# A mixer block on one core: another order for the first tiles, one tile transposed by DMA, one copied in halves

## The chip, the cores and the metric

The kernel runs on one core of a Trainium2 chip. The metric is the device time of one execution in microseconds; for the kernel before it is the median of three runs. A core has TensorE (PE, matmuls and transposes into PSUM), VectorE (DVE), ScalarE (ACT), GpSimd (POOL) and SyncE (SP, which here only issues DMAs). Each engine works through its own list of instructions in order and waits on semaphores for the others.

## The reference

One layer of an MLP-mixer on 2048 tokens of 512 channels, all bf16, cut to what matters:

```python
h  = gelu(layernorm(x) @ w1)                    # w1: 512 x 512
g0, g1, g2, g3 = four channel groups of h, shifted along the tokens by +1, -1, +2, -2
x1 = x + concat(g0, g1, g2, g3) @ w2            # w2: 512 x 512
out = x1 + gelu(layernorm(x1) @ w3) @ w4        # w3: 512 x 1792, w4: 1792 x 512
```

## The kernel before, in words

The tokens are split into 16 tiles of 128 (tile t holds the tokens 16p + t, one per partition p). A shift by one or two tokens is then mostly a neighbouring tile, so a tile of the second product needs hidden tiles up to two places away on either side. The second half of the kernel works in the order 8, 9, ..., 15, 0, ..., 7.

A matmul contracts over partitions, so each tile of x must be transposed (xnT) before the first product. There are two ways through the first layer:

- Raw tiles 0 to 5: the tile of x is transposed as it is, by PE (`tp`, four 128x128 transposes into PSUM, L323) with a copy by ScalarE (`ev`, L332), or, for tiles 4 and 5, by a transposing DMA from HBM (`tdma_x`, L351). Then four 128x512 matmuls (`m1r`, L378) and a ScalarE copy of the product to SBUF (`rc`, L388). The layer norm is put in later, from the column sums of w1 (`cs0` to `cs`, four 128x512 matmuls with a matrix of ones, L366, copied out by `cse`).
- Normalised tiles 6 to 15, in pairs: VectorE takes statistics (`st`, L289) and aggregates them (`ag`, L294), GpSimd takes the root (`rs`, L300), VectorE normalises (`nm`, L309). The pair is transposed by PE (pairs 8 and 10: `tp`, eight transposes, and one `ev` of 1024 columns) or by a transposing DMA from SBUF (pairs 6, 12, 14: `td0`, L343). Then 16 matmuls of 128x256 (`m1p`, L410) and a gelu by ScalarE (`g1p`, or `g1s` by single tiles for pair 10).

The second product (`m2`, L436 and L450) adds into x1 on VectorE (`x1`, L460); its parts for tiles 8 to 15 are cut into pieces by which hidden tiles they read. The third and fourth products (`m3h` L492, `m3` L468, `m4` L511) are long runs of PE work.

Ahead of everything PE runs a warm-up of matmuls on constants (`wu`, L534), while the first loads are under way.

What sets the order: a small `Program` class holds named operations with what they read and write. For each engine a list `firsts[...]` written out by hand gives the order of its first operations; those not named follow in the order in which they were added. `emit` derives the semaphore waits from reads and writes. SP's list matters as much as PE's: it issues nearly all loads and all transposing DMAs, in order, and an issue that waits for its data (`td0_6` waits for `nm0_6` and `nm0_7`) holds those behind it. PSUM has eight banks; a product can start only when the copy or gelu that emptied its bank is done.

Of the kernel before, what the change touches and what calls it, by code (L numbers as in the profile page):

```python
# [26 lines left out]
class Program:  # L27
# [7 lines left out]
    def add(self, eng, name, fn, reads=(), writes=(), dma=False):  # L35
        self.ops.append(Op(name, eng, fn, reads, writes, dma))
# [135 lines left out]
def bass_standalone__mixer_s_mlp__prompt_kernel(nc: bass.Bass, x, w1, w2, w3, w4, out):  # L172
# [4 lines left out]
    DC = D // P  # L177
# [5 lines left out]
    xd = x[0].rearrange("(p t) d -> p t d", t=NT)  # L183
# [4 lines left out]
    with ExitStack() as es:  # L188
        sb = lambda name, shape, dt: es.enter_context(nc.sbuf_tensor(name, shape, dt))
        x_sb = sb("x_sb", [P, NT, D], BF16)  # L190
# [3 lines left out]
        xnT = sb("xnT", [P, NT, DC, P], BF16)  # L194
# [21 lines left out]
        ones_wide = nc.const_aps.tensor(1.0, [P, 512], BF16)  # L216
# [66 lines left out]
        def dst_of(layer, t):  # L283
            return (xn, t, ("xn", t), 0) if layer == 0 else (x1n, POS[t] % 8, ("x1n", POS[t] % 8), t)
# [29 lines left out]
        def tp(t, n, b, raw):  # L314
            src = x_sb if raw else xn
            rd = [(("x", i), 0) if raw else (("xn", i), 0) for i in range(t, t + n)]

            def f(e):
                ins = None
                for i in range(n):  # L320
                    for c in range(DC):
                        o = 1024 * b + (i * DC + c) * P
                        ins = e.transpose(psb[:, o : o + P], src[:, t + i, P * c : P * (c + 1)], ident[:])  # L323
# [12 lines left out]


        def tdma(layer, t, n):
# [3 lines left out]
            add("sp", f"td{layer}_{t}",  # L342
                lambda e: e.dma_start(dst[:, p0 : p0 + n, :, :].rearrange("p t c s -> p (t c) s"),  # L343
                                      src[:, k : k + n, :].rearrange("p t d -> p (t d)"), transpose=True),
                reads=[dst_of(layer, i)[2:] for i in range(t, t + n)],
                writes=[(("xT", i) if layer == 0 else ("x1T", i), 0) for i in range(t, t + n)], dma=True)


        def tdma_x(t):
            add("sp", f"tdx_{t}",  # L350
                lambda e: e.dma_start(xnT[:, t : t + 2, :, :].rearrange("p t c s -> p (t c) s"),  # L351
                                      xd[:, t : t + 2, :].rearrange("p t d -> p (t d)"), transpose=True),
                writes=[(("xT", i), 0) for i in (t, t + 1)], dma=True)
# [20 lines left out]
        def m1r(t, b, c0=0, c1=DC):  # L374
            def f(e):
                ins = None
                for c in range(c0, c1):
                    ins = e.matmul(bank(b), xnT[:, t, c, :], w1_sb[:, c, :], start=(c == 0), stop=(c == DC - 1))  # L378
                return ins

            rd = [(("xT", t), 0)] + W1[c0:c1]
            if c0:
                rd += bres(b, 1, f"m1r{t}{c0}")
            end = f"{c1}" if c1 < DC else ""
            add("pe", f"m1r{t}{end}", f, reads=rd, writes=bres(b, 1, f"m1r{t}{end}"))

        def rc(t, b):
            add("act", f"rc{t}", lambda e: e.activation(yraw[:, t, :], bank(b), ACT_F.Copy),  # L388
                reads=bres(b, 1, f"m1r{t}"), writes=[(("yraw", t), 0)])
# [140 lines left out]
        def warmup(name, n, b):  # L530
            def f(e):
                ins = None
                for _ in range(n):
                    ins = e.matmul(bank(b), ones, ones_wide, start=True, stop=True)  # L534
                return ins

            add("pe", name, f, writes=bres(b, 1, name))
# [5 lines left out]
                writes=[(("w1", c), 0)], dma=True)  # L543

        def load_w2(c):
            add("sp", f"ldw2{c}", lambda e: e.dma_start(w2_sb[:, c, :], w2[P * c : P * (c + 1), :]),
                writes=[(("w2", c), 0)], dma=True)

        def load_w3a(c):
            add("sp", f"ldw3a{c}",  # L550
# [11 lines left out]
        load_w1(2, "act")  # L562
        load_w1(3, "sp")
        load_x(1, 1, "act")
        for t, n in ((6, 1), (7, 1), (2, 1), (8, 1), (3, 1), (9, 1), (10, 1), (11, 1), (12, 1), (13, 1), (14, 2), (4, 2)):
            load_x(t, n)
        for c in range(DC):
            load_w2(c)
        for c in range(DC):
            load_w3a(c)  # L570
        load_w3b()

        warmup("wu", 7, 5)
        YB = (0, 1, 2, 3, 0, 1)
        for c in range(DC):
            colsum(4, c)
        colsum_out(4)
        for t in range(R):
            if t < 4:
                tp(t, 1, 6 + t % 2, True)  # L580
                ev(t, 1, 6 + t % 2, "act")
            elif t == 4:
                tdma_x(t)
            cuts = [0, 1, 2, 3, 4] if t == 0 else [0, 2, 4] if t == 1 else [0, 4]
            for c0, c1 in zip(cuts, cuts[1:]):
                m1r(t, YB[t], c0, c1)
            rc(t, YB[t])
# [7 lines left out]
        for t in range(R, NT, 2):  # L595
# [2 lines left out]
                ev(t, 2, 6 + t // 2 % 2)  # L598
            else:
                tdma(0, t, 2)  # L600
        for t, b in ((6, 2), (8, 4), (10, 0), (12, 2), (14, 6)):
            m1p(t, b)
            if t == 10:
                g1s(t, b, 0)
                g1s(t, b, 1)
            else:
                g1p(t, b)
# [19 lines left out]
        for t in (8, 10):  # L627
# [7 lines left out]
            tdma(1, t, 2)  # L635

        firsts = {}
        firsts["pe"] = """wu tp0 cs0 cs1 m1r01 m1r02 tp1 m1r03 cs2 m1r0 cs tp2 m1r12 m1r1 tp3 m1r2 m1r3 m1r4 m1r5 tp8 m1p6
            tp10 m1p8 m1p10 m2_8a m2_9a m2_8 m2_9b m2_9 m2_10a m2_11a m2_12a m2_13a m1p12 m1p14 m2_10 m2_11
            m2_12b m2_13b m2_14a m2_15a m2_12 m2_13 m2_14b m2_15b m2_14 m2_15""".split()  # L640
        firsts["act"] = """ldw10 ldw12 ldx1 table ev0 ev1 rc0 ev2 ev3 rc1 rc2 rc3 rc4 rc5 ev8 cse g1p6 ev10 g1p8 g1s10 g1s11
            g1r0 g1r1 g1p12 g1p14 g2h_0_0_0 g2h_0_0_4 g1r2 g1r3 g2h_0_0_8 g2h_0_0_12 g1r4 g1r5""".split()
        firsts["dve"] = """pada padb padc padd pade padf st0_0 st0_6 st0_7 ag0_6 ag0_7
            st0_8 nm0_6 nm0_7 st0_9 ag0_8 ag0_9 st0_10 st0_11 nm0_8 nm0_9 ag0_10 ag0_11
            st0_12 nm0_10 nm0_11 st0_13 ag0_12 ag0_13 st0_14 st0_15 ag0_14 ag0_15 nm0_12 nm0_13 st0_1 ag0_0 ag0_1
            nm0_14 nm0_15 zr0 zr1 x1_8 x1_9 st1_8 st1_9 ag1_8 ag1_9 st0_2 nm1_8 nm1_9 st0_3 ag0_2 ag0_3 x1_10 x1_11 st1_10
            st1_11 ag1_10 ag1_11 x1_12 nm1_10 nm1_11 x1_13 x1_14 x1_15 zr2 zr3 st0_4 st0_5 ag0_4 ag0_5 zr4 zr5
            st1_12 st1_13 ag1_12 ag1_13""".split()
        firsts["pool"] = """ident0 ident1 neghalf stz ste rs0_6 rs0_8 rs0_10
            rs0_12 rs0_14 rs0_0 rs1_8 rs0_2 rs1_10""".split()  # L650
        firsts["sp"] = """ldx0 ldw11 ldx6 ldw13 ldx7 ldx2 ldx8 ldx3 ldx9 tdx_4 ldx10 ldx11 ldx12 td0_6 ldx13 ldx14 ldw20 ldw21 ldw22 ldw23 td0_12 td0_14 ldw3a0 ldw3a1
            ldw3a2 ldw3a3 th_0 td1_8 ldw3b ldx4 td1_10 th_2 th_4 td1_12 td1_14 ldw4""".split()

        slots = [4, 0, 2]
        ns = [0]
# [54 lines left out]
        for i, t in enumerate((0, 1, 2, 3, 4, 5, 6, 7)):  # L710
            b = (6, 7, 1)[i % 3]
# [54 lines left out]
```

## Time and profile before

| what | us |
|---|---|
| median of 3 runs | 136.76 (136.42, 136.76, 136.97) |
| the profiled execution | 136.32 |
| its span, first to last instruction | 134.5 |
| PE busy | 130.8 (97%) |
| VectorE busy | 58.3 (43%) |
| ScalarE busy | 46.8 (35%) |
| GpSimd busy | 12.5 (9%) |

The profiled execution is the only one of which the order of work in time is known; it was 0.44 us faster than the median. Busy time of PE includes the drain of each matmul, so 97% says that PE has hardly a pause, not that each matmul is at its fastest. A matmul is recorded with the time to its end (0.38 us for 128x512), while the next one starts one slot later (0.216 us). A few matmul records are missing from the trace. Times inside the span count from its start.

### The profile page before, as it was taken

The numbers are of one execution on the slowest core, as the hardware profiler recorded it, in microseconds if no ns is written. First come the engines' busy times: TensorE is split into PE (matmuls) and PEld (weight loads), VectorE is DVE, ScalarE is ACT, GpSimd is POOL, SyncE is SP. The second block draws the span as 40 slices with busy tenths as digits, with TensorE's granted clock in tenths as the row PEclk, the third lists the DMA queues.
The fourth block names the chain that finished last, engine by engine and source line by source line (L and its number), as shares of the span: only waits on it lengthen the run. The fifth ranks groups of instructions, "written<-read, shape, count | busy, mean of one in ns | idle before, by whom it ended". The sixth has DMA issues, their size and how long they took to land.

```text
span 134.5 us, 1794 instructions
## 1 busy us (share of the span) xinstructions
PE 130.8 (97%) x719; PEld 69.6 (52%) x729; DVE 58.3 (43%) x135; ACT 46.8 (35%) x56; POOL 12.5 (9%) x25
## 2 busy tenths in 40 slices
PE   7999999999999999999999999999999999999993
PEld 2446857678884444444444444444444444444452
DVE  0689999799967777762222000122200002322222
ACT  3488871507962036550001555200066630000000
POOL 2042422220330012220000000000000000000000
PEclk9999999999999999999999999999999999999999
DMA  4999379984465984444121000011110001111121
GB/s 123 317 247 217 115 145 246 255 292 83 78 128 100 295 262 78 78 80 78 39 68 49 5 0 0 0 39 39 41 37 5 0 0 39 39 39 39 44 75 42
DMA packets 24376, 12.96 MB, mean 96 GB/s; under 512 B 16688, under 2 KB 23600, under 8 KB 24368
## 3 DMA queue, kind: packets, MB, share of 16 engines
q1 hardware_dynamic: 23792, 12.42, 36.5%
q10 hardware_dynamic: 576, 0.43, 1.0%
q8 instruction: 6, 0.10, 0.3%
q14 instruction: 2, 0.02, 0.1%
HBM read 6.82 MB, written 2.10 MB: 66 GB/s over the span
## 4 chain that ended last, share of the span: by engine, by line
PE 89%; SPq 4%; DMA 2%; DVE 2%; issue 1%
PE ps L511 36%; PE ps L468 27%; PE ps L492 9%; PE ps L410 7%; PE ps L436 5%; PE ps L450 5%; DMA x_sb<-in_x_dram 2%; SPq L272 2%; SPq L351 1%; DVE st L289 1%; PE ps L323 1%; SPq L542 1%; DVE xn L309 0%; DVE o_sb L523 0%
## 5 line engine op out<-in xcount | busy, mean ns | idle before, releaser
L511 PE MATMUL ps<-w_sb,h2T 128*128 128x512 bf16 (+2 forms) x232 | 48.1, 366 | 0.3
L523 DVE TENSOR_TENSOR o_sb<-ps,x_sb 128x512 bf16<-128x512 f32 (+2 forms) x17 | 11.2, 660 | 61.2 <-PE ps L511 61.2
L479 ACT ACTIVATE h2T<-ps 128x1024 bf16<-128x1024 f32 x21 | 21.5, 1023 | 46.2 <-PE ps L468 46.2
L468 PE MATMUL ps<-x1nT,w_sb 128*128 128x512 bf16 x168 | 36.7, 379 | 0.0
L511 PEld LDWEIGHTS ps<-w_sb,h2T 128*128 128x128 bf16 x238 | 22.8, 98 | 25.9
L468 PEld LDWEIGHTS ps<-x1nT,w_sb 128*128 128x128 bf16 x168 | 16.4, 98 | 19.8
L289 DVE BATCH_NORM_STATS2 st<-x_sb 128x6 f32<-128x512 bf16 x32 | 20.9, 682 | 4.1 <-DMA x_sb<-in_x_dram 4.0
L300 POOL TENSOR_TENSOR rstd<-mv,neghalf 128x2 f32<-128x2 f32 x16 | 11.6, 725 | 46.1 <-DVE mv L294 46.1
L492 PE MATMUL ps<-x1nT,w_sb 128*128 128x256 bf16 x112 | 12.4, 273 | 0.0
L492 PEld LDWEIGHTS ps<-x1nT,w_sb 128*128 128x128 bf16 x112 | 11.0, 98 | 1.5
L460 DVE TENSOR_TENSOR x_sb<-ps,x_sb 128x512 bf16<-128x512 f32 x16 | 10.6, 685 | 2.5 <-PE ps L436 1.5
L410 PE MATMUL ps<-xnT,w_sb 128*128 128x256 bf16 x80 | 9.2, 273 | 0.0
L503 ACT ACTIVATE h2T<-ps 128x1024 bf16<-128x1024 f32 (+1 forms) x8 | 7.1, 913 | 6.0 <-PE ps L492 6.0
L410 PEld LDWEIGHTS ps<-xnT,w_sb 128*128 128x128 bf16 x80 | 7.6, 98 | 1.2
L309 DVE TENSOR_SCALAR x1n<-x_sb,mv,rstd 128x512 bf16<-128x512 bf16 x16 | 5.9, 409 | 5.3 <-POOL rstd L300 5.3
L450 PE MATMUL ps<-w_sb,hTf 128*128 128x512 bf16 x30 | 7.0, 379 | 0.1
L436 PE MATMUL ps<-w_sb,hTf 128*128 128x512 bf16 x31 | 6.9, 379 | 0.1
L378 PE MATMUL ps<-w_sb,xnT 128*128 128x512 bf16 x23 | 6.0, 382 | 0.1
L420 ACT ACTIVATE hTf<-ps 128x1024 bf16<-128x1024 f32 x4 | 4.1, 1023 | 4.2 <-PE ps L410 4.2
L332 ACT ACTIVATE xnT<-ps 128x512 bf16<-128x512 bf16 (+1 forms) x6 | 4.4, 738 | 2.3 <-PE ps L323 2.2
L436 PEld LDWEIGHTS ps<-w_sb,hTf 128*128 128x128 bf16 x32 | 3.1, 98 | 3.6
L294 DVE BATCH_NORM_AGGREGATE mv<-st 128x2 f32<-128x9 f32 x32 | 5.0, 185 | 0.0
(28 smaller groups left out, 36.8 us busy)
## 6 DMA issues: line engine op xcount, KB each, us to landing
out_dram<-o_sb SPq DMA_DIRECT2D x15, 128.0 KB, 1.8
w_sb<-in_w_dram SPq DMA_DIRECT2D x1, 1792.0 KB, 7.7
x_sb<-in_x_dram SPq DMA_DIRECT2D x11, 128.0 KB, 3.3
w_sb<-in_w_dram SPq DMA_DIRECT2D x4, 256.0 KB, 4.2
w_sb<-in_w_dram SPq DMA_DIRECT2D x6, 128.0 KB, 3.5
w_sb<-in_w_dram SPq DMA_DIRECT2D x1, 768.0 KB, 4.8
x_sb<-in_x_dram SPq DMA_DIRECT2D x2, 256.0 KB, 4.4
w_sb<-in_w_dram ACTq DMA_DIRECT2D x2, 128.0 KB, 3.2
```

Of the source, the lines that this page charges most:

```text
L289: add("dve", f"st{layer}_{t}", lambda e: e.bn_stats(st9[:, i, 0:6], src[:, t, :]), reads=[(r, 0)], writes=[(("st6", i), 0)])
L300: lambda e: e.tensor_tensor(rstd[:, i : i + n], mv[:, i : i + n, 1], neghalf[:, 0:n], ALU.pow),
L410: ins = e.matmul(dst, w1_sb[:, c, P * fc : P * (fc + 1)], xnT[:, t : t + 2, c, :], start=(c == 0), stop=(c == DC - 1))
L436: ins = e.matmul(bank(b), hTf[:, c0 : c0 + P], w2_sb[:, j, :], start=(j == 0), stop=(j == DC - 1))
L450: ins = e.matmul(bank(b), hTf[:, w[0] : w[0] + P], w2_sb[:, j, :], start=first and n == 0, stop=last and n == len(js) - 1)
L460: lambda e: e.tensor_tensor(x1_sb[:, t, :], bank(b), x_sb[:, t, :], ALU.add),
L468: ins = e.matmul(bank(b), w3_sb[:, c, P * fc : P * (fc + 1)], x1nT[:, 4 * q : 4 * q + 4, c, :], start=(c == 0), stop=(c == DC - 1))
L479: lambda e: e.activation(h2T[:, fc : fc + 2, q % 2, :], src, ACT_F.Gelu_apprx_tanh),
L492: ins = e.matmul(dst, w3_sb[:, c, P * (fc + i) : P * (fc + i + 1)], x1nT[:, t : t + 2, c, :], start=(c == 0), stop=(c == DC - 1))
L503: lambda e: e.activation(h2T[:, fc : fc + n, q % 2, 256 * k : 256 * (k + 1)], src, ACT_F.Gelu_apprx_tanh),
L511: ins = e.matmul(ps[:, 512 * b : 512 * b + c1 - c0], h2T[:, fc, q % 2, P * i : P * (i + 1)], w4_sb[:, fc, c0:c1], start=(fc == 0), stop=(f ...
L523: lambda e: e.tensor_tensor(o_sb[:, k % 4, c0:c1], ps[:, 512 * b : 512 * b + c1 - c0], x1_sb[:, t, c0:c1], ALU.add),
```

## The change

In words:

- The warm-up is 14 matmuls of 256 columns instead of 7 of 512.
- Tile 0 is transposed and copied in two halves (`tp0a`/`ev0a` into bank 6, `tp0b`/`ev0b` into bank 7); its first two matmuls read only the first half.
- Tile 3 is transposed by a DMA from HBM of its own (`tdx_3`), ahead of the one for tiles 4 and 5. Its own load (`ldx3`, still wanted by the statistics and by x1) moves behind pair 14's transpose.
- Tiles 8 and 9 are loaded ahead of 6 and 7; pair 8 is normalised first, transposed behind `m1r3`, and multiplied (`m1p8`) ahead of pair 10's transposes and of `m1p6`. The PSUM banks of the two products are exchanged.
- The last column sum (`cs`) moves from behind `m1r0` to behind `m1r2`; tile 1's transposes stand behind `m1r03`.
- Tiles 12 and 13 are one load, 14 and 15 two; tile 15's comes right behind pair 6's transpose. w2 comes in two loads instead of four. Two of the four first parts of w3 are issued ahead of pair 12's transpose.

```diff
+        def tp_part(t, c0, c1, b, part, res):
...
+            add("pe", f"tp{t}{part}", f, reads=[(("x", t), 0), ("ident", 1)], writes=bres(b, 1, f"tp{t}{part}"))
+            add("act", f"ev{t}{part}",
+                lambda e: e.activation(xnT[:, t, c0:c1, :].rearrange("p c s -> p (c s)"), psb[:, o : o + n], ACT_F.Copy),
+                reads=bres(b, 1, f"tp{t}{part}"), writes=[(res, 0)])
...
-            rd = [(("xT", t), 0)] + W1[c0:c1]
+            rd = [(("xTa", t) if t == 0 and c1 <= 2 else ("xT", t), 0)] + W1[c0:c1]
...
-                    ins = e.matmul(bank(b), ones, ones_wide, start=True, stop=True)
+                    ins = e.matmul(ps[:, 512 * b : 512 * b + 256], ones, ones_wide, start=True, stop=True)
...
-        for t, n in ((6, 1), (7, 1), (2, 1), (8, 1), (3, 1), (9, 1), (10, 1), (11, 1), (12, 1), (13, 1), (14, 2), (4, 2)):
+        for t, n in ((8, 1), (6, 1), (7, 1), (2, 1), (3, 1), (9, 1), (10, 1), (11, 1), (12, 2), (14, 1), (15, 1), (4, 2)):
             load_x(t, n)
-        for c in range(DC):
+        for c in range(0, DC, 2):
             load_w2(c)
...
-        warmup("wu", 7, 5)
+        warmup("wu", 14, 5)
...
-            if t < 4:
+            if t == 0:
+                tp_part(0, 0, 2, 6, "a", ("xTa", 0))
+                tp_part(0, 2, 4, 7, "b", ("xT", 0))
+            elif t < 3:
                 tp(t, 1, 6 + t % 2, True)
                 ev(t, 1, 6 + t % 2, "act")
-            elif t == 4:
-                tdma_x(t)
+            elif t < 5:
+                tdma_x(t, 1 if t == 3 else 2)
...
-        for t, b in ((6, 2), (8, 4), (10, 0), (12, 2), (14, 6)):
+        for t, b in ((6, 4), (8, 2), (10, 0), (12, 2), (14, 6)):
...
-        firsts["pe"] = """wu tp0 cs0 cs1 m1r01 m1r02 tp1 m1r03 cs2 m1r0 cs tp2 m1r12 m1r1 tp3 m1r2 m1r3 m1r4 m1r5 tp8 m1p6
-            tp10 m1p8 m1p10 m2_8a m2_9a m2_8 ...
+        firsts["pe"] = """wu tp0a tp0b cs0 cs1 m1r01 m1r02 m1r03 tp1 m1r0 cs2 tp2 m1r12 m1r1 m1r2 cs m1r3 tp8 m1r4 m1r5
+            m1p8 tp10 m1p6 m1p10 m2_8a m2_9a m2_8 ...
-        firsts["act"] = """ldw10 ldw12 ldx1 table ev0 ev1 rc0 ev2 ev3 rc1 rc2 rc3 rc4 rc5 ev8 cse g1p6 ev10 g1p8 g1s10 g1s11
+        firsts["act"] = """ldw10 ldw12 ldx1 table ev0a ev0b ev1 ev2 rc0 rc1 rc2 rc3 ev8 rc4 rc5 cse ev10 g1p8 g1p6 g1s10 g1s11
...
-        firsts["dve"] = """pada padb padc padd pade padf st0_0 st0_6 st0_7 ag0_6 ag0_7
-            st0_8 nm0_6 nm0_7 st0_9 ag0_8 ag0_9 st0_10 st0_11 nm0_8 nm0_9 ag0_10 ag0_11
-            st0_12 nm0_10 nm0_11 st0_13 ag0_12 ag0_13 st0_14 st0_15 ag0_14 ag0_15 nm0_12 nm0_13 st0_1 ag0_0 ag0_1
+        firsts["dve"] = """pada padb padc padd pade padf st0_0 st0_8 ag0_8 st0_9 ag0_9
+            st0_6 st0_7 ag0_6 ag0_7 nm0_8 nm0_9 nm0_6 nm0_7 st0_10 st0_11 ag0_10 ag0_11
+            st0_12 nm0_10 nm0_11 st0_13 ag0_12 ag0_13 st0_14 nm0_12 nm0_13 st0_15 ag0_14 ag0_15 st0_1 ag0_0 ag0_1
...
-        firsts["pool"] = """ident0 ident1 neghalf stz ste rs0_6 rs0_8 rs0_10
+        firsts["pool"] = """ident0 ident1 neghalf stz ste rs0_8 rs0_6 rs0_10
...
-        firsts["sp"] = """ldx0 ldw11 ldx6 ldw13 ldx7 ldx2 ldx8 ldx3 ldx9 tdx_4 ldx10 ldx11 ldx12 td0_6 ldx13 ldx14 ldw20 ldw21 ldw22 ldw23 td0_12 td0_14 ldw3a0 ldw3a1
-            ldw3a2 ldw3a3 th_0 td1_8 ldw3b ldx4 td1_10 th_2 th_4 td1_12 td1_14 ldw4""".split()
+        firsts["sp"] = """ldx0 ldw11 ldx8 ldw13 ldx9 ldx2 ldx6 ldx7 tdx_3 tdx_4 ldx10 ldx11 ldx12 ldx14 td0_6 ldx15 ldw20 ldw22 ldw3a0 ldw3a1 td0_12 td0_14 ldx3 ldw3a2
+            ldw3a3 th_0 td1_8 ldw3b ldx4 td1_10 th_2 th_4 td1_12 td1_14 ldw4""".split()
```

More of the change, by code (lines that the diff above doesn't have):

```diff
@@ L215, in bass_standalone__mixer_s_mlp__prompt_kernel @@
         ones = nc.const_aps.tensor(1.0, [P, P], BF16)
-        ones_wide = nc.const_aps.tensor(1.0, [P, 512], BF16)
+        ones_wide = nc.const_aps.tensor(1.0, [P, 256], BF16)
         one_f = nc.const_aps.tensor(1.0, [P, 1], F32)
@@ L335, in ev, with f @@
             add(eng, f"ev{t}", f, reads=bres(b, 1, f"tp{t}"), writes=[(("xT", i), 0) for i in range(t, t + n)])
+        def tp_part(t, c0, c1, b, part, res):
+            o = 1024 * b
+            n = (c1 - c0) * P
+            def f(e):
+                ins = None
+                for c in range(c0, c1):
+                    k = o + (c - c0) * P
+                    ins = e.transpose(psb[:, k : k + P], x_sb[:, t, P * c : P * (c + 1)], ident[:])
+                return ins
+            add("pe", f"tp{t}{part}", f, reads=[(("x", t), 0), ("ident", 1)], writes=bres(b, 1, f"tp{t}{part}"))
+            add("act", f"ev{t}{part}",
+                lambda e: e.activation(xnT[:, t, c0:c1, :].rearrange("p c s -> p (c s)"), psb[:, o : o + n], ACT_F.Copy),
+                reads=bres(b, 1, f"tp{t}{part}"), writes=[(res, 0)])
         def tdma(layer, t, n):
@@ L346, in tdma, with tdma_x @@
                 writes=[(("xT", i) if layer == 0 else ("x1T", i), 0) for i in range(t, t + n)], dma=True)
-        def tdma_x(t):
+        def tdma_x(t, n):
             add("sp", f"tdx_{t}",
-                lambda e: e.dma_start(xnT[:, t : t + 2, :, :].rearrange("p t c s -> p (t c) s"),
-                                      xd[:, t : t + 2, :].rearrange("p t d -> p (t d)"), transpose=True),
-                writes=[(("xT", i), 0) for i in (t, t + 1)], dma=True)
+                lambda e: e.dma_start(xnT[:, t : t + n, :, :].rearrange("p t c s -> p (t c) s"),
+                                      xd[:, t : t + n, :].rearrange("p t d -> p (t d)"), transpose=True),
+                writes=[(("xT", i), 0) for i in range(t, t + n)], dma=True)
         def tdma_h(t, n):
@@ L545, in load_w2 @@
         def load_w2(c):
-            add("sp", f"ldw2{c}", lambda e: e.dma_start(w2_sb[:, c, :], w2[P * c : P * (c + 1), :]),
-                writes=[(("w2", c), 0)], dma=True)
+            add("sp", f"ldw2{c}",
+                lambda e: e.dma_start(w2_sb[:, c : c + 2, :],
+                                      w2[P * c : P * (c + 2), :].rearrange("(c p) f -> p c f", p=P)),
+                writes=[(("w2", c + i), 0) for i in range(2)], dma=True)
         def load_w3a(c):
@@ L637, in bass_standalone__mixer_s_mlp__prompt_kernel @@
         firsts = {}
-        firsts["pe"] = """wu tp0 cs0 cs1 m1r01 m1r02 tp1 m1r03 cs2 m1r0 cs tp2 m1r12 m1r1 tp3 m1r2 m1r3 m1r4 m1r5 tp8 m1p6
-            tp10 m1p8 m1p10 m2_8a m2_9a m2_8 m2_9b m2_9 m2_10a m2_11a m2_12a m2_13a m1p12 m1p14 m2_10 m2_11
+        firsts["pe"] = """wu tp0a tp0b cs0 cs1 m1r01 m1r02 m1r03 tp1 m1r0 cs2 tp2 m1r12 m1r1 m1r2 cs m1r3 tp8 m1r4 m1r5
+            m1p8 tp10 m1p6 m1p10 m2_8a m2_9a m2_8 m2_9b m2_9 m2_10a m2_11a m2_12a m2_13a m1p12 m1p14 m2_10 m2_11
             m2_12b m2_13b m2_14a m2_15a m2_12 m2_13 m2_14b m2_15b m2_14 m2_15""".split()
-        firsts["act"] = """ldw10 ldw12 ldx1 table ev0 ev1 rc0 ev2 ev3 rc1 rc2 rc3 rc4 rc5 ev8 cse g1p6 ev10 g1p8 g1s10 g1s11
+        firsts["act"] = """ldw10 ldw12 ldx1 table ev0a ev0b ev1 ev2 rc0 rc1 rc2 rc3 ev8 rc4 rc5 cse ev10 g1p8 g1p6 g1s10 g1s11
             g1r0 g1r1 g1p12 g1p14 g2h_0_0_0 g2h_0_0_4 g1r2 g1r3 g2h_0_0_8 g2h_0_0_12 g1r4 g1r5""".split()
-        firsts["dve"] = """pada padb padc padd pade padf st0_0 st0_6 st0_7 ag0_6 ag0_7
-            st0_8 nm0_6 nm0_7 st0_9 ag0_8 ag0_9 st0_10 st0_11 nm0_8 nm0_9 ag0_10 ag0_11
-            st0_12 nm0_10 nm0_11 st0_13 ag0_12 ag0_13 st0_14 st0_15 ag0_14 ag0_15 nm0_12 nm0_13 st0_1 ag0_0 ag0_1
+        firsts["dve"] = """pada padb padc padd pade padf st0_0 st0_8 ag0_8 st0_9 ag0_9
+            st0_6 st0_7 ag0_6 ag0_7 nm0_8 nm0_9 nm0_6 nm0_7 st0_10 st0_11 ag0_10 ag0_11
+            st0_12 nm0_10 nm0_11 st0_13 ag0_12 ag0_13 st0_14 nm0_12 nm0_13 st0_15 ag0_14 ag0_15 st0_1 ag0_0 ag0_1
             nm0_14 nm0_15 zr0 zr1 x1_8 x1_9 st1_8 st1_9 ag1_8 ag1_9 st0_2 nm1_8 nm1_9 st0_3 ag0_2 ag0_3 x1_10 x1_11 st1_10
```

## Prediction, before the result was known

> **What bounds the kernel now.** I read the page's chain of waits by share first, then the chain in order of time, then the timeline of the first 18 us, and last the DMA view, the whole and in windows around single issues.
>
> ```profile
> PE 89%; SPq 4%; DMA 2%; DVE 2%; issue 1%
> ...
> 4.97 1.40 SPq L351
> 6.37 0.05 issue
> 6.42 3.24 DMA x_sb<-in_x_dram
> 9.66 0.02 issue
> 9.68 1.29 DVE st L289 x2
> 10.97 0.64 DVE xn L309 x2
> 11.61 0.05 issue
> 11.66 0.62 PE ps L323 x8
> 12.28 1.81 PE ps L410 x16
> 14.09 0.45 PE ps L323 x8
> 14.53 3.50 PE ps L410 x32
> ```
>
> The chain leaves TensorE (PE) once: SyncE's issues (SPq) up to tile 10's load, its landing at 9.66, its statistics, the normalising of pair 8, and at 11.66 pair 8's transposes. From there to 132 the chain is PE without a gap over 0.05 us. Whatever the change does after 12 us is free as long as its data come in time; what it can win lies in the first 12 us.
>
> ```profile
> 3.71 0.63 PE L323 MATMUL ps<-ident,x_sb 128*128 128x128 bf16 x4
> 4.14 1.06 PE L366 MATMUL ps<-w_sb,const-bfloat16-1.0 128*128 128x512 bf16 x2
> 7.70 0.39 PE L323 MATMUL ps<-ident,x_sb 128*128 128x128 bf16 x4
> 7.93 3.62 PE L378 MATMUL ps<-w_sb,xnT 128*128 128x512 bf16 x15
> 8.41 1.24 SPq L343 DMA_TRANSPOSE xnT<-xn  x1
> 11.65 0.45 PEld L323 LDWEIGHTS ps<-ident,xn 128*128 128x128 bf16 x8 [0.61 <-DVE xn L309]
> 12.16 1.92 PE L410 MATMUL ps<-xnT,w_sb 128*128 128x256 bf16 x16
> ```
>
> Prices from these rows: a warm 128x512 matmul has a slot of 0.216 us (chain: L468 x56 in 12.09), a 128x256 one 0.109 (x32 in 3.50), four 128x128 transposes 0.22 (7.70 to 7.93). Tiles 2 to 5 are 16 matmuls from 7.93 (one record is missing), so they end at 11.39; pair 8's transposes start at 11.66: PE stands still for 0.28. Pair 6's DMA transpose, issued at 8.41, lands after 3.7, at 12.12, and m1p6 starts at 12.16: no slack there either, 0.05 lost. m1p10 ends at 17.85.
>
> ```profile
> x_sb<-in_x_dram SPq DMA_DIRECT2D x11, 128.0 KB, 3.3
> xnT<-xn SPq DMA_TRANSPOSE x3, 3.2
> xnT<-in_x_dram SPq DMA_TRANSPOSE x1, 4.3
> ```
>
> These are the times from issue to landing that I use below.
>
> **The change part by part.**
>
> Warm-up: 7 matmuls of 512 columns become 14 of 256. The weight loads of the first 3.7 us start 0.43 apart, twice the later slot, so the array is at half speed there, and 14 x 0.213 = 7 x 0.427 = 2.99 us. Its weight loads of 0.15 hide in 0.213. Price 0; bounds -0.1 (tile 0 may start at 3.58 instead of 3.71, x0 having landed by 3.57) and +0.1.
>
> Tile 0 in halves: ScalarE copies 512 columns in 0.60 and 1024 in 1.02, so 256 take about 0.39. First half 4.18 to 4.57, second to 4.85, against one copy 4.38 to 4.98. But cs0 and cs1 occupy PE from 4.14 at 0.427 each, to 4.99; m1r01 began at 5.03. Gain 0.04; the colsums cover the rest.
>
> Tile 3: its four transposes go, -0.22 on PE, and one copy of 0.60 on ScalarE, off the path. In their place SP issues a transpose of one tile from HBM, ninth in its queue, at about 4.5. Its issue time and landing are not in the trace. Issue: between a load's 0.43 and the two-tile transpose's 1.40; I take 0.9, half-way. Landing: it queues behind tile 7, which will land near 7.5 to 7.8 (the loads in those two places, tiles 3 and 9, landed at 7.52 and 8.21), plus half of the 1.07 by which the two-tile transpose followed tile 9 (9.28 - 8.21): 8.1 to 8.4; the far bound is the whole 4.31, 8.8. [...] Pair 4's transpose comes at 5.4 instead of 4.97 and lands at 9.2 to 9.9.
>
> PE order, slot by slot: cs1 ends 4.99; m1r01 (part of it still slow, 0.28), m1r02, m1r03 to 5.75; tile 1 transposed to 5.98; m1r0 and cs2 to 6.41; tile 2 lands at 6.48, its transposes 6.52 to 6.75 (0.11 lost); m1r12 needs ev1, whose source is ready near 6.19 and which takes 0.60: 6.82 (0.08 lost). Before, m1r0 and two colsums lay between tile 1's transposes and this point, now less does. m1r1, m1r2, cs are 9 slots: 8.77. m1r3 wants tile 3 at 8.77 (slack 0.4 to 0.7 by the estimate, 0 at the far bound). 9.63 pair 8's transposes, m1r4 at 10.08, m1r5 ends 11.80, m1p8 13.55, pair 10's transposes 14.00, m1p6 15.74, m1p10 17.49.
>
> VectorE order (statistics 0.69, 0.60 behind another; two aggregates 0.32; roots on GpSimd 0.70; two norms 0.73): tile 8 takes tile 6's place (4.97), tile 9 tile 7's (5.89), aggregates done 6.83, roots 7.6; tiles 6 and 7 wait for their loads at 6.81 and 7.52; norms of 8 and 9 end near 9.2. Pair 8's transposes at 9.63 have 0.4 in hand, and the 0.28 wait is gone. The cost moves to pair 6: its roots 8.5 to 9.26, norms to 10.0, DMA transpose issued at 10.0 instead of 8.41, landing 3.1 to 3.7 later, 13.1 to 13.8; m1p6 wants it at 14.00. Slack 0.2 to 0.9. Tile 10's load is issued near 6.9, lands about 9.75 to 10.2; norms 10 and 11 end 13.0 to 13.3, wanted 13.55.
>
> ScalarE: pair 8's copy moves ahead of rc4, rc5: 10.3 to 11.35, m1p8 11.80. ev10 14.2 to 15.2, m1p10 15.74. g1p8, then g1p6, end 17.1; m2_8a wants them at 17.49. All covered by 0.4 or more, but if m1p6 is late, g1p6 and m2_8a are late with it one for one.
>
> SP: tile 15, w2 in two loads and two parts of w3 stand behind pair 6's transpose, which waits to 10.0. Last w2 issue near 12.4, plus about 3.8: 16.2, wanted 17.5. Pair 12's transpose, behind two w3 issues that end at 13.6, waits for its norms at 15.3 anyway (16.43 before). Pair 14's is issued near 17.7 (17.88 before), lands 21, wanted 22.7. Tile 3's own load comes behind it near 19, lands 22, in front of its statistics (23.54 before). The tail after m2_8a is the same list shifted.
>
> Sum at the end of m1p10: -0.22 (transposes) -0.28 -0.05 (waits gone) +0.19 (new waits at tiles 1 and 2), and the halves' 0.04 = -0.36 by rounding to rows (17.49 against 17.85). I carry -0.35. The profiled execution took 136.32, span 134.5 and 1.8 around it; it would give 135.97. It is 0.44 below the median of 136.76, so I apply the difference to the median: 136.4. A measurement of this kernel can tell about 0.5% (0.68 us) from no change, so the forecast is within it.
>
> **The rivals.**
>
> Late clock. PE is at half speed to about 5.2 us in this execution. [...] As a mechanism here: 1 us more at half speed delays PE by 0.5, and the 0.28 wait at pair 8 was then hidden before, while the new list has almost no wait to hide it in. The gain shrinks to 0.05 to 0.2: about 136.65. For it: the 0.55 spread of the runs.
>
> Longer waits in the median run. The profiled run is the fastest shown; if the others lost 0.44 at the two places without slack (pair 8, pair 6), the new list with some 0.4 there saves that too: 0.35 + 0.44 = 0.8, 136.0. Against it: nothing shows where the other runs lost.
>
> Tile 3 late (slower). Each 0.1 that tile 3 lands after 8.77 holds PE for 0.1. From 9.1 the gain is used up; from 9.8 the kernel is slower by over 0.68, 137.45. The longest landing of a small transpose is 5.0 (after 21.2, behind 1 MB of w3): 9.5 here, 0.7 lost, 137.1; if the two transposes in a row also push pair 4 and tile 10 back, pair 10's norms and with them m1p6 lose up to 0.5 more: 137.6. For it: a transpose from HBM was the slowest small transfer before 13 us at 4.3. Against: one tile is half of it.
>
> The change does what it says in all orders; only the halves of tile 0 bring next to nothing.
>
> **How the numbers follow.** Forecast 0.52 (136.4, its own range 136.1 to 136.7); late clock 0.15 (136.65); longer waits 0.17 (136.0); tile 3 late 0.16 (137.0 to 137.6). Faster by over 0.5% (below 136.08): 0.13 of the longer waits and 0.05 of the forecast's edge, 0.18. Slower (above 137.44): a good half of tile 3 late, 0.10, and 0.05 for a wait I priced by the wrong row, 0.15. The rest is 0.67. The range reaches over the longer waits' 136.0 and tile 3's milder half: 135.8 to 137.2.
>
> **What would show it.** Right: no L323 transposes of raw tiles after 7 us; pair 8's transposes at 9.6 without a VectorE wait; m1p6 at 14.0; the first L467 matmul (L450 before) at 17.5; nothing new after it. Wrong: a wait on a DMA ahead of m1r3 or m1r4 (tile 3's or pair 4's landing after 8.8 or 10.1), ahead of m1p6 (pair 6 after 14.0), or a PE gap behind 18 us, which would mean that I mis-sized a slack in the tail.

## The result

| | median us | runs | profiled execution |
|---|---|---|---|
| before | 136.41 (136.25 to 136.97) | 22 | 136.32, span 134.5 |
| after | 136.71 (136.37 to 137.06) | 22 | 136.48, span 134.6 |

The ratio after to before is 1.0018, 95% interval [1.001, 1.0025]: the change costs 0.25 us. The forecast was a gain of 0.35 us, applied to the median of the three runs shown, 136.76; beside the 22 runs that median was high, and the profiled execution (136.32) lay near the true one. Against the 136.41 the forecast's difference has the wrong sign and is 0.6 us off. The measured 136.71 lies inside the forecast's 135.8 to 137.2, but that is the width of the range and the luck of a high base, not the reasoning: on 136.41 the forecast would have read 136.06.

The first line of the page's part on the chain that ended last, changed kernel:

```profile
PE 93%; DMA 3%; SPq 2%; issue 0%; DVE 0%
```

VectorE's share is gone. The chain in order of time (start, length, what), changed kernel:

```profile
2.60 0.43 SPq L272
3.04 0.04 issue
3.08 3.91 DMA x_sb<-in_x_dram
6.99 0.05 issue
7.04 0.40 PE ps L323 x4
7.43 1.73 PE ps L395 x8
9.16 0.22 PE ps L383
9.38 0.86 PE ps L395 x4
10.24 0.45 PE ps L323 x8
10.69 1.73 PE ps L395 x8
12.41 1.75 PE ps L427 x16
14.16 0.45 PE ps L323 x8
14.61 3.49 PE ps L427 x32
18.10 3.45 PE ps L467 x16
```

The chain leaves PE now at 6.99, at the landing of tile 2, instead of at 11.61 at the norms of pair 8. From 7.04 on PE has no pause. (The chain goes by the drained ends of the matmuls; the next one's record starts 0.16 earlier, as the rows below show.) Pair 8's transposes follow `m1r3` at once (10.08), m1p6 (the x32 row is m1p6 and m1p10) starts at 14.45 without a wait, the second product at 17.94. By its drained end m1p10 ends at 18.10; before it was 14.53 + 3.50 = 18.03. What follows is the same list: the execution's time less this end is 136.48 - 18.10 = 118.38 here and 136.32 - 18.03 = 118.29 before. What the change lost lies ahead of 7.04.

The timeline of the changed kernel, PE and SyncE (start, length, engine, line, operation; idle time before it and what ended it in brackets):

```profile
5.92 0.40 PE L323 MATMUL ps<-ident,x_sb 128*128 128x128 bf16 x4 [0.40 <-DMA x_sb<-in_x_dram]
7.04 0.40 PE L323 MATMUL ps<-ident,x_sb 128*128 128x128 bf16 x4 [0.28 <-DMA x_sb<-in_x_dram]
4.50 2.62 SPq L368 DMA_TRANSPOSE xnT<-in_x_dram  x2
10.61 1.24 SPq L360 DMA_TRANSPOSE xnT<-xn  x1
10.08 0.61 PE L323 MATMUL ps<-ident,xn 128*128 128x128 bf16 x8
14.45 3.66 PE L427 MATMUL ps<-xnT,w_sb 128*128 128x256 bf16 x32
17.94 1.24 PE L467 MATMUL ps<-w_sb,hTf 128*128 128x512 bf16 x5
```

The brackets count from the drained end of the matmul before; counted by slots PE stands still 0.56 ahead of tile 1's transposes and 0.45 ahead of tile 2's. Tile 1 landed at 5.88 (5.13 before), tile 2 at 6.99 (6.48). PE's slots (0.213 for 256 columns at first, 0.109 later) narrowed near 3.45 in this execution instead of 5.19. That is worth at most 0.87 of PE time, half of the difference, and the waits ate it: these two, and 0.29 ahead of the second column sum, for the second part of w1 (landed 4.44).

Both profiled executions lie below the median of their kernel (136.32 and 136.41, 136.48 and 136.71), so the two traces show 0.16 of the difference, which is 0.25 by the ratio and 0.30 by the medians.

### The profile page after: what moved, and what is told of

Same layout as the page of the kernel before. It is cut to its first block, busy times and chain, and to the rows that moved or that the text cites. A ratio compares the mean times of both kernels' runs of the same rounds, so it can differ in the third digit from the quotient of the medians.

```text
span 134.6 us, 1809 instructions
## 1 busy us (share of the span) xinstructions
PE 130.7 (97%) x732; PEld 70.1 (52%) x732; DVE 58.3 (43%) x135; ACT 46.0 (34%) x56; POOL 12.5 (9%) x25
## 4 chain that ended last, share of the span: by engine, by line
PE 93%; DMA 3%; SPq 2%; issue 0%; DVE 0%
PE ps L528 36%; PE ps L485 27%; PE ps L509 9%; PE ps L427 6%; PE ps L453 5%; PE ps L467 5%; PE ps L395 3%; DMA x_sb<-in_x_dram 3%; PE ps L323 1%; SPq L272 1%; SPq L559 1%; DVE o_sb L540 0%; PE ps L383 0%
## 5 line engine op out<-in xcount | busy, mean ns | idle before, releaser
L528 PE MATMUL ps<-w_sb,h2T 128*128 128x512 bf16 (+2 forms) x238 | 48.9, 366 | 0.0
L453 PEld LDWEIGHTS ps<-w_sb,hTf 128*128 128x128 bf16 x32 | 3.1, 98 | 3.6
L467 PEld LDWEIGHTS ps<-w_sb,hTf 128*128 128x128 bf16 x32 | 3.1, 97 | 3.4 <-ACT hTf L442 0.2
```

The lines of the kernel that those rows point to most:

```text
L453: ins = e.matmul(bank(b), hTf[:, c0 : c0 + P], w2_sb[:, j, :], start=(j == 0), stop=(j == DC - 1))
L467: ins = e.matmul(bank(b), hTf[:, w[0] : w[0] + P], w2_sb[:, j, :], start=first and n == 0, stop=last and n == len(js) - 1)
L528: ins = e.matmul(ps[:, 512 * b : 512 * b + c1 - c0], h2T[:, fc, q % 2, P * i : P * (i + 1)], w4_sb[:, fc, c0:c1], start=(fc == 0), stop=(f ...
```

## The experiments

Ratios are against the kernel before, run beside each. The question in three groups: do PE's order, tile 3 or the clock make the loss; does tile 2's place in SyncE's queue; do the tiles that are loaded third and fifth. A diff shows only the part of a list that differs. Each kernel has one trace.

### PE's order, tile 3, the warm-up

e1, changed kernel, with PE's first tiles in the order of before:

```diff
- tp0a tp0b cs0 cs1 m1r01 m1r02 m1r03 tp1 m1r0 cs2 tp2 m1r12 m1r1 m1r2 cs m1r3
+ tp0a tp0b cs0 cs1 m1r01 m1r02 tp1 m1r03 cs2 m1r0 cs tp2 m1r12 m1r1 m1r2 m1r3
```

> The changed kernel with only PE's order of the first tiles as it was before: tile 1's transposes ahead of m1r03, and the last column sum ahead of tile 2's transposes. Theory 'filler': PE now stands 0.58 us before tile 1's transposes (5.35 to 5.92) and 0.45 before tile 2's (6.59 to 7.04), because work that used to lie there was moved behind them; with it back (two matmuls, 0.43 us), tile 2's wait is filled with cs, and the time falls by 0.2 to 0.4, to a ratio of 0.9985 to 1.000 against the kernel before. Theory 'tile 3' (the extra transposing DMA costs): no change, ratio 1.001 to 1.0025. Theory 'warm-up': no change either.

Measured: 1.0014 [0.9997, 1.0031]. In its trace tile 1 landed at 6.07, tile 2 at 7.46; m1p10 ended at 18.35. The old order alone brings nothing that the interval can tell from 1.0018. The work put back between the two tiles did fill tile 2's wait in the trace: PE waited 0.49 for tile 1, but reached tile 2's transposes only when the tile was there. Its slots narrowed only near 6.69, which also delayed it.

e2, changed kernel, tile 3 on PE again (`tp3` behind `m1r1`, its copy, its load in `tdx_3`'s place):

> The changed kernel with tile 3 back on PE (transposes tp3, copy ev3, its load where its DMA transpose stood). Theory 'tile 3': in the profile after, the transpose took 1.27 us to issue and landed at 8.58, and pushed tiles 4/5's to 9.62 and tile 10's load to 10.13; without it the loads of tiles 10 to 15 come 0.6 to 0.8 earlier, the time falls by 0.2 or more although PE has 0.22 more to do: ratio 0.999 to 1.000. Theory 'filler': PE waits for tiles 1 and 2, not for tile 3 (m1r3 followed cs without a gap), so the time rises by the 0.22 of transposes: ratio 1.002 to 1.004.

Measured: 1.0024 [1.001, 1.0037]. Tile 3's DMA is not the loss. The 0.22 that its four transposes cost on PE cannot be seen in the medians either: 0.0006 is 0.08 us. It is in the trace: from the start of tile 2's transposes to the end of m1p10 it takes 11.29 (7.09 to 18.38), in the changed kernel 11.06 (7.04 to 18.10).

e3, kernel before with the warm-up of 14 x 256; e4, changed kernel with that of 7 x 512:

```diff
- warmup("wu", 7, 5)     # e3: 14 of 256; e4 the other way
+ warmup("wu", 14, 5)
```

> The kernel before with only the warm-up changed to 14 matmuls of 256. Theory 'warm-up' (the form of the warm-up moves the moment at which the clock rises: 3.4 us in the profile after, 5.2 before): the clock rises at about 3.4 here too, and the time moves by 0.1 or more. Theories 'filler' and 'tile 3': the moment is a matter of the single execution, the time stays within 0.1: ratio 0.9995 to 1.0005.

> The changed kernel with the warm-up back at 7 matmuls of 512. Theory 'warm-up': the clock rises near 5.2 and the time moves by 0.1 or more from the changed kernel's 1.0018. Theories 'filler' and 'tile 3': ratio 1.001 to 1.0025 as the changed kernel.

Measured: e3 1.0007 [0.9997, 1.0016], e4 1.0023 [1.0002, 1.0044]. PE's slots narrowed at 5.30 and 3.61. Over all traces that moment lies between 3.45 and 6.69 us: the warm-up's form doesn't make the loss, and in these two traces it doesn't set the moment. e3 shows something else, in two rows of its timeline (kernel before, other warm-up) and one of its chain:

```profile
6.01 0.40 PE L323 MATMUL ps<-ident,x_sb 128*128 128x128 bf16 x4 [0.26 <-DMA x_sb<-in_x_dram]
11.87 0.61 PE L323 MATMUL ps<-ident,xn 128*128 128x128 bf16 x8
```

```profile
14.68 3.50 PE ps L410 x32
```

Tile 1 landed at 5.96 here, 0.83 later than in the trace of before. Its transposes started 0.48 later (6.01 for 5.53), pair 8's 0.21 later (11.87 for 11.66), and m1p10 ended 0.15 later (14.68 + 3.50 = 18.18 for 18.03). The waits for pair 8's norms (0.28) and for pair 6's transpose (0.05) are gone in this trace: the list before hides most of a late tile 1 in them. The changed list has no such place: what tiles 1 and 2 lose early is lost.

### Tile 2's place in the queue

e5 and e6, changed kernel, one place earlier and one later; e7 and e17, the kernel before, one later and one earlier:

```diff
- ldx8 ldw13 ldx9 ldx2 ldx6 ldx7        (changed kernel)
+ ldx8 ldw13 ldx2 ldx9 ldx6 ldx7        e5
+ ldx8 ldw13 ldx9 ldx6 ldx2 ldx7        e6
- ldx6 ldw13 ldx7 ldx2 ldx8             (kernel before)
+ ldx6 ldw13 ldx7 ldx8 ldx2             e7
+ ldx6 ldw13 ldx2 ldx7 ldx8             e17
```

> The changed kernel with tile 2's load one place earlier on SP, ahead of tile 9's. Theory 'tile 2 is the bound' (in the changed list PE has no wait from tile 2's transposes on, so the end follows tile 2's landing one for one): tile 2 lands about 0.35 earlier, its transposes start at 6.6 to 6.8, the first second-layer matmul at 17.5 to 17.8 instead of 17.94 to 18.2, time 0.2 to 0.35 less than the changed kernel: ratio 0.999 to 1.0005. Tile 9 lands 0.35 later and has the slack. Theory 'later part' (the loss lies behind 18 us or in the order as a whole): no change, ratio 1.001 to 1.0025.

> The changed kernel with tile 2's load one place later, behind tile 6's. Theory 'tile 2 is the bound': transposes at 7.4 to 7.8, time 0.3 to 0.4 more than the changed kernel: ratio 1.004 to 1.005. Theory 'later part': no change, 1.001 to 1.0025.

> The kernel before with tile 2's load one place later, behind tile 8's: the same shift as in e6, in the other list. Theory 'tile 2 is the bound': the list before has two column sums ahead of tile 2 and waits for pair 8's norms later (0.28 at 11.66), so it is less sensitive: 0 to 0.2 more, ratio 1.000 to 1.0015. Theory 'all lists alike': 0.35 more, 1.0025.

> The kernel before with only tile 2's load one place earlier, ahead of tile 7's. If the gain of the last run is nothing but this place in the queue: ratio 0.998 to 0.999. If the rest of the change is needed for it, because in the list before pair 8's norms and pair 6's transpose end the first 12 us: no gain, 0.9995 to 1.001, with tile 7's statistics and pair 6's transpose 0.3 us later and m1p6 waiting for it.

Measured: e5 1.0005 [0.9992, 1.0018], e6 1.003 [1.0014, 1.0046], e7 1.0012 [1.0002, 1.0023], e17 1.0017 [1.0008, 1.0027]. In the changed list a place is worth 0.0012 to 0.0013, some 0.17 us, in both directions by the middle of the intervals; those of e5 and e6 still overlap a little, and e6 lost less than the 1.004 expected. The single traces don't show it as cleanly: tile 2 landed at 7.31 in e6, but at 7.00 in e5, where tile 1 was late too (6.28). In the list before either move costs; why the earlier place costs there is not settled. Tile 7 is later for it, but the trace of e17 shows no wait for pair 6; PE's slots narrowed only near 6.4 in that execution, and it waited nowhere after.

e8, changed kernel with tile 2's load two places earlier, ahead of w1's last part, and PE's order made for it:

```diff
- ldx8 ldw13 ldx9 ldx2      PE: m1r03 tp1 m1r0 cs2 tp2 m1r12 m1r1
+ ldx8 ldx2 ldw13 ldx9      PE: m1r03 tp1 cs2 tp2 m1r12 m1r0 m1r1
```

> A version drawn from the theory: the changed kernel with tile 2's load two places earlier (ahead of w1's last part, which then lands 0.35 later), and on PE cs2, tile 2's transposes and m1r12 ahead of m1r0, the only early user of that part. Theory 'tile 2 is the bound': transposes at 6.3 to 6.6, time 0.3 to 0.6 less than the changed kernel, below the kernel before: ratio 0.997 to 0.9995; from about 6.9 on the bound is tile 3's DMA transpose (8.6 to 8.9) or pair 8's norms. Theory 'later part': no change, 1.001 to 1.0025.

Measured: 1.0045 [1.0027, 1.0063]. A miss: tile 1 landed at 6.85, PE waited 1.5 us for it.

### Which pair is first

e9, changed kernel with pair 6 loaded, normalised and multiplied first, as before:

> The changed kernel with one part undone: pair 6 again ahead of pair 8, in the loads (tiles 6 and 7 in the third and fifth place on SP, 8 and 9 behind tile 2), on VectorE, ScalarE and PE, and in the banks. The rest (warm-up, halves, tile 3 by DMA, cs and tile 1's order, the loads behind) stays. Seven executions with tile 8 in the third place had tile 1 landing at 5.6 to 6.9 (mean 6.05), three with tile 6 there at 5.1 to 6.0 (mean 5.5), so: theory 'order of loads' (tile 8 in third place makes the next loads land later): tile 1 lands at 5.1 to 6.0, tile 2 at 6.4 to 6.9, its transposes by 6.95; pair 8's norms are late as before (near 11.2), so pair 8's transposes follow m1r5 with little wait, and the time is 0.2 to 0.4 less than the changed kernel: ratio 0.999 to 1.000. Theory 'chance' (the landings scatter in every kernel): tile 1 anywhere from 5.1 to 6.9, and the time as the changed kernel's or above, 1.0015 to 1.0035, since the wait for pair 8's norms is back.

Measured: 1.009 [1.0069, 1.0111], the largest effect of all and above both expectations. Tile 1 landed at 5.54 and tile 2 at 6.94. Its timeline (SyncE's and PE's rows):

```profile
9.21 1.24 SPq L360 DMA_TRANSPOSE xnT<-xn  x1
12.31 0.62 PE L323 MATMUL ps<-ident,xn 128*128 128x128 bf16 x8 [0.39 <-DVE xn L309]
13.84 0.39 PE L427 MATMUL ps<-xnT,w_sb 128*128 128x256 bf16 x2 [0.91 <-DMA xnT<-xn]
```

Pair 8's transposes wait for its norms, and m1p6 0.91 for pair 6's transpose, issued at 9.21 behind more loads and landed at 13.79. With tile 3 by DMA and the loads moved up, "pair 8 first" is what keeps these two waits away.

### Which tiles are loaded third and fifth

e12, changed kernel with tiles 8 and 9 exchanged; e13, the kernel before with only the loads of 8, 9 and 6, 7 exchanged (a single run; pair 6 is then late):

```diff
- ldx0 ldw11 ldx8 ldw13 ldx9 ldx2     (changed kernel)
+ ldx0 ldw11 ldx9 ldw13 ldx8 ldx2     e12
- ldx0 ldw11 ldx6 ldw13 ldx7 ldx2     (kernel before)
+ ldx0 ldw11 ldx8 ldw13 ldx9 ldx2     e13
```

> The changed kernel with tiles 8 and 9 exchanged in their places on SP (9 third, 8 fifth) and in the order of their statistics. Theory 'order of loads', if only the neighbour of tile 0 counts: tile 1 lands near 5.5, tile 2 near 6.8, time 0.2 to 0.4 less, ratio 0.9985 to 1.0005. If both tiles of the pair are slow next to 0 and 1: as the changed kernel, 1.001 to 1.0025. Theory 'chance': as the changed kernel.

> The kernel before with nothing changed but four loads: 8 and 9 in the third and fifth place on SP and 6 and 7 in theirs. Its time is of no use (pair 6's norms wait for tile 7 until about 8.2, which should cost 1 us or more); looked at are the loads. Theory 'order of loads': between 4.0 and 5.5 us it moves 230 to 320 GB/s as the seven executions with tile 8 in third place did, not 320 to 353 as the four with tile 6 there; tile 1 lands after 5.55. Theory 'chance' or 'something else in the changed kernel': 320 to 353, tile 1 before 5.55.

Measured: e12 1.0018 [1.0007, 1.0029], tile 1 at 6.54, tile 2 at 7.42. e13 138.13 us, 295 GB/s from 4.0 to 5.5 us, tile 1 at 6.05, tile 2 at 7.26.

e10 and e11, the loads by themselves, in 12 groups of three orders (A: 6 third, 7 fifth; B: 8 and 9; C: that of e8) and in 16 groups of four pairs (A, B; H: 9 and 8; E: 10 and 11), each group waiting for the one before:

> Loads alone: twelve groups of ten loads of 128 KB, each group issued when the one ahead has landed, nothing computed (the products are left out, the output is a copy of tiles of x). A has the order of the kernel before (tiles 0, 6, 7, 2, 8 with two parts of w1 between, and on ScalarE's queue two parts of w1 and tile 1), B that of the changed kernel (0, 8, 9, 2, 6), C that of e8 (0, 8, 2, then w1, 9, 6). Theory 'order of loads': tile 1 lands 0.3 to 0.7 later after its issue in B than in A, and later still in C, in every group. Theory 'chance': no difference between A, B and C beyond their scatter.

> Loads alone again (nothing computed, the output is a copy of a few tiles): sixteen groups of nine loads, four of each of four orders that differ only in the two tiles at the third and fifth place on SP: 6 and 7 (A), 8 and 9 (B), 9 and 8 (H), 10 and 11 (E). In the run of loads before this one the 1.5 us from 3.26 after a group's start moved 321 to 357 GB/s in A and 197 to 332 in B. Theory 'order of loads': B again near 280, A near 340; if it is the distance of 8 tiles from tiles 0 and 1 that matters, H is as slow as B and E as fast as A. Theory 'chance': all four alike, near 310.

Measured, GB/s in the same 1.5 us of each group: e10 A 345, 352, 357, 321; B 307, 332, 294, 197; C 262, 291, 250, 288. e11 A 295, 335, 277, 315; B 321, 291, 270, 259; H 337, 314, 280, 287; E 329, 335, 293, 311. B is below A in both (means 344 and 283, 306 and 285), but the ranges overlap in both. Tile 1's landing after its issue, which was to be 0.3 to 0.7 later in B in every group of e10, is later by 0.07 in the mean (4.01 for 3.94) and by 0.11 in e11 (4.01 for 3.90), in a scatter from 3.5 to 4.6. Inconclusive.

Over the 18 traces of whole kernels, one execution each, the picture is clearer. The windows view from 4.0 to 5.5 us (window, length, busy time of PE, PEld, DVE, ACT, POOL, clock, DMA share, GB/s), kernel before:

```profile
4.00:5.50 1.50, 1.50 (x8) 0.52 (x6) 0.79 (x2) 0.60 (x1) 0.00 (x0) 1.00 1.07 353
```

The same, changed kernel:

```profile
4.00:5.50 1.50, 1.38 (x8) 0.35 (x5) 0.42 (x1) 0.66 (x2) 0.00 (x0) 1.00 0.94 284
```

With tile 6 third (7 traces) the rate is 320 to 372 GB/s, and tile 1 lands at 5.54 in the mean (5.13 to 5.96); with tile 8 or 9 third (11 traces) it is 232 to 345, and tile 1 lands at 6.06 (5.53 to 6.85). SyncE's sixth load (tile 2's in both lists) lands at 6.64 and 7.21 in the mean. Only two of the 11 reach the lowest rate of the seven.

e14 puts it to the test inside the changed kernel: tiles 6 and 7 loaded third and fifth, 8 and 9 next, pair 8 still multiplied first. e15 has tile 2 one place earlier as well.

```diff
- SP: ldx0 ldw11 ldx8 ldw13 ldx9 ldx2 ldx6 ldx7      PE: m1r2 cs m1r3 tp8 m1r4 m1r5 m1p8
+ SP: ldx0 ldw11 ldx6 ldw13 ldx7 ldx2 ldx8 ldx9      PE: m1r2 m1r3 m1r4 tp8 m1r5 cs m1p8
+ SP of e15: ldx0 ldw11 ldx6 ldw13 ldx2 ldx7 ldx8 ldx9
```

> The changed kernel with tiles 6 and 7 loaded third and fifth again and 8 and 9 seventh and eighth (statistics, roots and norms in that order too), pair 8 still multiplied first, but its transposes behind m1r4 instead of m1r3 and the last column sums of w1 between m1r5 and m1p8. Order of loads decides: tile 1 lands near 5.5 and tile 2 near 6.7, PE reaches pair 8's transposes at 10.5 when its norms (10.4) are ready, m1p8 starts near 12.0 instead of 12.41, and the end comes 0.3 to 0.4 us earlier than in the changed kernel: ratio to before 0.998 to 0.999. If it doesn't matter which tiles are third and fifth: tile 1 near 6, tile 2 near 7, m1p8 at 12.4, ratio 1.001 to 1.002. If pair 8's later load costs more than I work out (norms after 10.8): a wait on VectorE ahead of pair 8's transposes, ratio above 1.002.

> The same, and tile 2's load one place earlier, ahead of tile 7's. Order of loads: tile 2 near 6.3, a further 0.17 us as in the two runs that moved this load, as far as the norms of pair 8 (10.4) allow: then the wait moves to pair 8's transposes and the ratio is that of the run before, 0.998 to 0.999, at best 0.997. If it doesn't matter which tiles are third and fifth: 1.000 to 1.001.

Measured: 1.0012 [1.0, 1.0024] and 1.0011 [0.9998, 1.0025]. The loads came as expected (371 and 372 GB/s, tile 1 at 5.51 and 5.40, tile 2 at 6.61 and 6.13, pair 8's norms at 10.22 in e14), the gain did not. The chain of e14:

```profile
5.82 3.93 DMA xnT<-in_x_dram
9.75 0.05 issue
9.80 1.04 PE ps L395 x4
10.83 0.45 PE ps L323 x8
11.28 0.86 PE ps L395 x4
12.14 0.22 PE ps L383
12.36 0.04 issue
12.40 1.92 PE ps L427 x16
```

Pair 4's transpose lands at 9.75, little later than in the changed kernel (9.62), and my order had moved `m1r4`, which reads it, ahead of `tp8`: PE was free for it at 9.58 and waited 0.22. It waited another 0.20 ahead of `m1p8` (12.40) for ScalarE's copy of pair 8's transposes, which now had five matmuls to hide behind instead of eight. e15's trace has the same two waits (0.21 and 0.20) and one of 0.19 for tile 3's transpose.

### Cover and place together

Cover is the work that PE has between tile 1's transposes and tile 2's.

e16, changed kernel with both PE's order of e1 and tile 2's place of e5; e18, the same with tile 3 on PE again, as in e2:

> The changed kernel with tile 2's load ahead of tile 9's and the PE order of the first tiles as it was before the change (m1r03 and two column sums between tile 1's and tile 2's transposes). The two runs that did one of the two each gave 1.0005 and 1.0014. Order of loads: tiles 8 third and 9 sixth still land late, so about 1.000 (0.999 to 1.001), not below the kernel before by what can be measured. If the PE order was the loss: 0.999 or less.

> The kernel of the last run (PE order of the first tiles as before the change, tile 2's load one place earlier; 136.36, 0.9986) with tile 3 transposed on TensorE again. If that kernel is free of waits from the first column sums on, as its trace shows, then every PE instruction counts and the four transposes cost the 0.22 us of the forecast's term: ratio 1.0002 (0.9995 to 1.001). If waits for loads still decide in the middling execution, the transposes lie in them as they did in the changed kernel (1.0024 against 1.0018): ratio 0.9986 to 0.999.

Measured: e16 136.36 us, 0.9986 [0.9973, 1.0]; e18 1.0012 [1.0001, 1.0024]. e16 is the only kernel below the one before, and its interval still touches 1.0; it is clear of the changed kernel's [1.001, 1.0025]. Its chain:

```profile
1.20 3.53 DMA w_sb<-in_w_dram
4.73 0.05 issue
4.78 0.39 PE ps L383
5.17 0.43 PE ps L395 x2
5.60 0.38 PE ps L323 x4
5.97 0.22 PE ps L395
6.19 0.22 PE ps L383
6.41 0.22 PE ps L395
6.62 0.22 PE ps L383
6.84 0.22 PE ps L323 x4
7.06 2.59 PE ps L395 x12
9.65 0.57 PE ps L323 x8
10.22 1.73 PE ps L395 x8
11.95 1.75 PE ps L427 x16
13.69 0.51 PE ps L323 x8
14.20 3.49 PE ps L427 x32
```

From 4.78 on the chain stays on PE; by slots PE pauses 0.14 ahead of tile 1's transposes and 0.11 ahead of pair 8's, for its norms. Four matmuls (0.87 us) lie between the two sets of transposes, and tile 2 had landed at 6.23, 0.7 behind tile 1. m1p10 ends at 17.69, 0.34 below the 18.03 of before: the forecast's sum, in a kernel without the waits at tiles 1 and 2. (Tile 1 came early in this execution, at 5.53; by the medians e16 gains 0.2.) e18 costs 0.0026 more, 0.35 us, with intervals that just do not overlap. How much of it is the transposes' 0.22 isn't shown: in the trace of e18 PE also waited 1.17 for tile 1 (landed 6.17) and 0.27 for tile 3's load (landed 8.63, transposes at 8.67).

e1 alone gave 0.0004 and e5 alone 0.0013 against the changed kernel, both together 0.0032. That they add up to more than their sum lies within the intervals.

## Why the prediction was wrong

**The step that failed** is the term "+0.19 (new waits at tiles 1 and 2)". It took tile 1's landing (5.13) and tile 2's (6.48) from the one trace of before and kept them through a change that rewrites the queue which brings them. 5.13 is the earliest of all 18 traces. In the changed kernel tile 2 landed at 6.99 and its transposes started at 7.04 instead of 6.52, 0.52 late. The second product started at 17.94 instead of 17.49, 0.45 late: the whole miss lies here. From tile 2's transposes on, the forecast's 17.49 - 6.52 = 10.97 stands against 17.94 - 7.04 = 10.90; the 0.08 that it gave to a wait for ev1 did not come. In place of the 0.19 PE stood 0.56 and 0.45 ahead of the two tiles; that is more than the 0.52 that counts because its slots narrowed early and it reached them sooner. (The terms as written there add up to -0.40, not -0.36; the -0.35 is the difference of the two ends, so nothing hangs on it.)

That the end follows tile 2's landing one for one shows in the four traces whose lists are the same behind it:

| | tile 2 lands | m1p10 ends | the execution |
|---|---|---|---|
| changed kernel | 6.99 | 18.10 | 136.48 |
| e4 | 7.04 | 18.15 | 136.55 |
| e6 | 7.31 | 18.42 | 136.79 |
| e12 | 7.42 | 18.52 | 136.81 |

m1p10 ends 11.10 to 11.11 after the landing, and 118.3 to 118.4 follow. An estimate from this: with tile 2 at 7.21, the mean of SyncE's sixth load in the 11 traces with tile 8 or 9 third, the time is 7.21 + 11.11 + 118.37 = 136.69, beside the measured median of 136.71; with 6.48 it is 135.96. In the seven traces with tile 6 third the mean is 6.64. So of the 0.73 between 6.48 and 7.21, 0.16 is that the one trace was an early one, and 0.57 is the difference between the two groups of traces.

**What stood behind it** was seen and not drawn out: the forecast says that "now less does" lie between tile 1's transposes and tile 2's, and priced it at the landings of that trace. The price of lost cover is the spread of the landing, not its value in one execution. Before, a tile 1 that was 0.83 late cost 0.15 at m1p10's end (e3); after, the end follows tile 2's landing. e16 shows the rest: with the cover back and tile 2 a place earlier the gain appears. The forecast also left out w1's last part, which `m1r0` reads right behind tile 1's transposes in the new order: in e2, e4 and e9 PE stood 0.45 to 0.49 there for it (it landed at 6.22 to 6.34, in the trace of before at 5.50).

**The landings themselves** are later in the mean with tile 8 or 9 third, by about half a microsecond. The traces support that it goes with the tiles that stand third and fifth; e13 and e14, which exchange them in either kernel, moved as it says, in one execution each. That the order of tiles is the cause isn't shown: e14 and e15 got the early landings back and lost them to other waits, and e16, with tile 8 third, had them early too (345 GB/s, tile 1 at 5.53). Why tiles 8 and 9 should come slower isn't known; e10 and e11 have the sign but not the size (tile 1 later by 0.07 and 0.11).

**Point by point.** Right: both waits at pairs 8 and 6 gone; pair 8's transposes without a VectorE wait (10.08, forecast 9.63, late with tile 2); pair 6's transpose issued at 10.61 and landed at 13.85 (forecast 10.0 and 13.1 to 13.8), wanted at 14.45; tile 3 in time (landed 8.58, a little behind the 8.1 to 8.4 of the forecast and inside its far bound of 8.8, wanted 9.21), so the rival "tile 3 late" did not come; the warm-up and tile 0's halves at next to nothing; no new wait after 18 us. The -0.22 for tile 3 is in the traces (e2's stretch behind tile 2 is 0.23 longer), not in the medians of e2.

Mis-sized without effect: the issue of the one-tile transpose took 1.27, not 0.9, near the upper bound of 1.40. Two tiles took 1.30 in the same trace, so the issue hardly depended on the size.

The rival "late clock" had the right reasoning, that the new list has no wait left to hide a delay in, and the wrong delay: in the profiled execution PE's slots narrowed early, and the loads were late. That the moment differs from execution to execution was the author's assumption there, which the one trace of before did not show; over the traces of the experiments it lay between 3.45 and 6.69. "Longer waits in the median run" fell with its premise, the high median of three runs.

## What to carry to other kernels

A list that waits at one late place has slack at all earlier ones; taking that wait away makes every earlier landing count, so cost the landings by their spread over executions and not by the one trace at hand. When the order of the first loads is changed, forecast their landings anew and see what work lies between two that PE waits for: here two more matmuls of cover and one place in a queue turned a loss of 0.25 us into a gain of 0.2. A part that shows nothing in the medians when it is undone (tile 3 in e2) can still be read in a trace, over a stretch in which PE never waits.

## What the hardware showed

- The first loads scatter: tile 1, third of three issues on ScalarE's queue at 1.66 to 1.67 us in every kernel, landed between 5.13 and 6.85 in 18 traces. A load lands in 16 parts (16 landing records for each, in the traces of before and after), and what waits for it starts behind the last: in the changed kernel tile 2's parts came between 6.00 and 6.99, its transposes started at 7.04. In e12 fifteen parts of tile 1 were there at 5.49 and the last at 6.54, in the kernel before all came between 4.63 and 5.13.
- The DMA rate from 4.0 to 5.5 us was 320 to 372 GB/s with tile 6 third in SyncE's queue and 232 to 345 with tile 8 or 9, loads of the same size and shape. Loads alone (e10, e11) did not separate the two.
- A transpose of one tile from HBM cost SyncE 1.27 us of issue in the changed kernel, one of two tiles 1.30 there and 1.40 in the kernel before (at most 1.69, in e17), a plain load of 128 KB 0.43.
- The moment when PE's slots narrow (from 0.427 to 0.216 us for 512 columns, from 0.213 to 0.109 for 256) varied from about 3.45 us (changed kernel) to 6.69 (e1), over 3.2 us, among kernels with the same start but for the form of the warm-up; these two have the same warm-up. What sets the moment is not shown.
